# Normalising all tokens before modulating them, and projecting the last queries late, in a fused adaLN attention and feed-forward kernel

## The chip, the cores and the metric

The kernel runs on one core of a Trainium2 chip. The metric is the device time in microseconds. An execution has a few parts per thousand of scatter, so times are medians of three to eleven runs. A core has TensorE (PE in the profile, PEld for its weight loads), ScalarE (ACT), VectorE (DVE), GpSimd (POOL) and SyncE (SP, which here only issues DMA).

## The reference, cut to what matters

```python
# x: 2048 tokens x 1024, 32 heads of 32, one shared key/value head, feed-forward width 3584
mod = (silu(c) @ w_mod)                       # six rows: sa, ca, ga, sb, cb, gb
h = layernorm(x) * (1 + ca) + sa
x = x + ga * attention(h, wq, wk, wv, wo)     # softmax over 2048 keys
h = layernorm(x) * (1 + cb) + sb
x = x + gb * ((silu(h @ w1) * (h @ w3)) @ w2)
```

## The kernel before

The program builds a graph of instructions, and a list scheduler in Python orders it per engine from hand-set durations. The order on each engine is then fixed.

The queries are handled in five blocks, 256, 256, 512, 512 and 512 queries (blocks 0 to 4). In each block, attention is a stream of scores on TensorE, exponentials of 128x1024 on ScalarE (1024 in the whole kernel), and sums over values on TensorE. The score matmuls of one exponential are called a score group. The feed-forward of a block runs on TensorE, with its tanh on ScalarE, under the attention of the next block. That of block 4 runs alone at the end.

The prologue works by token blocks of 512 and interleaves them with the first attention:

```python
for tb in range(NTB):                          # 4 token blocks of 512
    for i in range(4): ln_stats(tb * 4 + i)    # VectorE
    ln_scale(tb * 4, 4)                        # GpSimd, 128x4
    for i in range(4): ln_norm(tb * 4 + i, q0 + i)         # VectorE: (x - mean) * rs
    ...
    ln_transpose(4, q0, HT of tb, ..., 0, 1, ("act", "dve") if tb < 2 else ("dve",))
                                               # TensorE transposes; the eviction from PSUM modulates
    kv(tb)
    if tb == 0: qproj(0, 0)
...
for f in range(1, NC): qproj(0, f)
...
for tb in range(1, NTB):
    for f in range(NC): qproj(tb, f)           # all queries during blocks 0 and 1
```

The softmax here doesn't subtract the row's maximum and nothing guards it: scores larger than these inputs give would overflow.

Of the kernel before, what the change touches and what calls it, by code (L numbers as in the profile page):

```python
# [8 lines left out]
P = 128  # L9
# [10 lines left out]
class Group:  # L20
    def __init__(self):
        self.bank = None
        self.nodes = []


class Dag:
# [71 lines left out]
    def schedule(self, banks):  # L98

        t_free = {e: 0.0 for e in ENGS}  # L100
# [27 lines left out]
        def free_banks():  # L128
            out = []
            for b in banks:  # L130
                if b in closed:
                    continue
                g = bank_group[b]
                if g is None:
                    out.append((0.0, b))
                elif all(x.start is not None for x in g.nodes):
                    out.append((max(x.vis for x in g.nodes), b))
            return sorted(out)

        while left:  # L140
            best = None
            for e in ENGS:
# [3 lines left out]
                fb = free_banks() if e == "pe" else None  # L146
                cands = []
                tmin = None
                for n in ready[e]:
                    est = n.est  # L150
                    if n.acq is not None:
                        if not fb:
                            continue
                        est = max(est, fb[0][0] + SEM_LAT)
# [17 lines left out]
            if e == "pe":  # L172
                att = mode in ("S", "V")

                def key(c):
                    s, n = c
                    if n.cls == "S":
                        r = 0
                    elif n.cls is not None:
                        r = 1 if att or t - n.est > 1.0 else 4  # L180
                    else:
                        r = 3
                    return (r, n.prio, n.seq)
            elif e == "dve":
                def key(c):
                    s, n = c
                    p = n.prio
                    if t - n.est > 4.0:
                        p -= 3
                    return (p, n.seq)  # L190
# [6 lines left out]
            if n.acq is not None:  # L197
                fb = free_banks()
# [123 lines left out]
def build(nc, x_in, wq_in, wk_in, wv_in, wo_in, w1_in, w3_in, w2_in, c_in, wmod_in, out, S, D, F):  # L322
# [15 lines left out]
    NTR = 5  # L338
    NXS = 8
# [16 lines left out]
    WKR = sb("WKR", [P, NC, 4, 32], BF16)  # L356
# [9 lines left out]
    RS = sb("RS", [P, NT], F32)  # L366
    NHALF = sb("NHALF", [P, 4], F32)

    HT = HREG[:].rearrange("p (c s) -> p c s", c=NC)
    HHT = HREG[:, 0:NF * 512].rearrange("p (f s) -> p f s", f=NF)  # L370
    o = NF * 512
    TS = HREG[:, o:o + 512]
    TT = HREG[:, o + 512:o + 1024]
    O2B = HREG[:, o + 1024:o + 2048].rearrange("p (a t d) -> p a t d", a=2, t=2)
    HKEY = "HREG"
# [20 lines left out]

    def grp():
        return Group()
# [21 lines left out]
    xload(0, 8)  # L420
    for k in range(NC):
        dma(lambda e, k=k: e.dma_start(WM01[:, k, :], wmod_in[k * P:(k + 1) * P, 0:2 * D]), ("wm01", k),
            writes=[("UR", k)], nbytes=P * 2 * D * 2)
    dma(lambda e: e.dma_start(WKV[:, 0], wk_in.rearrange("(c p) f -> p c f", p=P)), "wk", writes=WKK, nbytes=65536)
    dma(lambda e: e.dma_start(WKV[:, 1], wv_in.rearrange("(c p) f -> p c f", p=P)), "wv", writes=WVK, nbytes=65536)
    WQK = [("WREG", "q")]
    dma(lambda e: e.dma_start(WQ[:, :, 0:P], wq_in[:, 0:P].rearrange("(c p) f -> p c f", p=P)), "wq0",
        writes=[("WQ", 0)] + WQK, nbytes=P * D * 2)

# [16 lines left out]
    g = grp()  # L446
    for k in range(NC):
        def mm(e, k=k, g=g):
            for j in range(16):
                i = e.matmul(PB[g.bank][:, j:j + 1], WM01[:, k, j * P:(j + 1) * P], SCT[:, k:k + 1],  # L450
                             start=(k == 0 and j == 0), stop=True, skip_group_check=True)
            return i
        G.add("pe", mm, reads=["SCT", ("UR", k)], dur=16 * 0.06, lat=0.2, acq=g if k == 0 else None,
              groups=[(g, "w")], mode="F")
    G.add("dve", lambda e, g=g: e.tensor_copy(MODC[:, 0, :], PB[g.bank][:, 0:8]), writes=[("MODC", 0)],
          groups=[(g, "r")], dur=0.13, prio=0)
    G.add("dve", lambda e, g=g: e.tensor_scalar(MODC[:, 1, :], PB[g.bank][:, 8:16], 1.0, None, ALU.add),
          writes=[("MODC", 1)], groups=[(g, "r")], dur=0.13, prio=0)
    G.add("pool", lambda e: e.tensor_copy(WKR[:], WKV[:, 0].unsqueeze(2).broadcast_to([P, NC, 4, 32])), reads=WKK,
          writes=["WKR"], dur=1.3)  # L460

    def ln_stats(t):
        s, q = t % NXS, t % 4
        for a in range(2):
# [3 lines left out]
              reads=[("ST", q, 0), ("ST", q, 1)], writes=[("MV", t)], dur=0.15, prio=2)  # L468

# [7 lines left out]
    def xnt(q):  # L477

        return XN[:, q, :] if q < 4 else UREG[:, (NU + NTR - 2) * 2048 + (q - 4) * D:][:, 0:D]

    def xnk(q):
        return [] if q < 4 else [("UR", NU + NTR - 2 + (q - 4) // 2)]

    def ln_norm(t, q):
        s = t % NXS
        G.add("dve", lambda e: e.tensor_scalar(xnt(q), X[:, s, :], MV[:, t, 0:1], RS[:, t:t + 1],
                                               ALU.subtract, ALU.mult),
              reads=[("X", s), ("RS", t), ("MV", t)], writes=[("XN", q)] + xnk(q), dur=0.42, prio=2)
# [31 lines left out]

    def mm_group(n, f, reads_f, n_cols=512, per=1, prio=5, late=0):
# [13 lines left out]
    def kv(tb):  # L535
        sl = slice(tb * 512, (tb + 1) * 512)
        hk = lambda c: [("HT", c, tb), HKEY]
        g = mm_group(NC, lambda e, b, c: e.matmul(b, WKR[:, c].rearrange("p a f -> p (a f)"), HT[:, c, sl],
                                                  start=c == 0, stop=c == NC - 1), lambda c: ["WKR"] + hk(c))
        G.add("dve", lambda e, g=g: e.tensor_copy(KT[:, sl], PB[g.bank]), writes=[("KT", tb)], groups=[(g, "r")],  # L540
              dur=dve_t(512), prio=1)

        def vmm(e, b, i):
            tt, c = i // NC, i % NC
            return e.matmul(b[:, tt * 32:(tt + 1) * 32], HT[:, c, tb * 512 + tt * P:tb * 512 + (tt + 1) * P],
                            WKV[:, 1, c, :], start=c == 0, stop=c == NC - 1)
        g = mm_group(4 * NC, vmm, lambda i: WVK + hk(i % NC), n_cols=128, per=NC)
# [4 lines left out]
    def qproj(tb, f):  # L552
        sl = slice(tb * 512, (tb + 1) * 512)
        g = mm_group(NC, lambda e, b, c: e.matmul(b, WQ[:, c, f * P:(f + 1) * P], HT[:, c, sl],  # L554
                                                  start=c == 0, stop=c == NC - 1),
                     lambda c: [("WQ", min(f, 1)), ("HT", c, tb), HKEY] + WQK)
        G.add("dve", lambda e, g=g: e.tensor_copy(QT[:, f, sl], PB[g.bank]),  # L557
              writes=qkeys(f, tb * 512, 512), groups=[(g, "r")], dur=dve_t(512), prio=1)

# [3 lines left out]
    for tb in range(NTB):  # L563
        for i in range(4):
            ln_stats(tb * 4 + i)
        ln_scale(tb * 4, 4)
        q0 = 4 if tb == 1 else 0
        for i in range(4):
            ln_norm(tb * 4 + i, q0 + i)
        if tb + 2 < NTB:  # L570
            xl = xload(tb * 4 + 8, 4)
        ln_transpose(4, q0, lambda c, tb=tb: HT[:, c, tb * 512:(tb + 1) * 512],
                     lambda c, tb=tb: [("HT", c, tb)], 0, 1, ("act", "dve") if tb < 2 else ("dve",))
        kv(tb)
        if tb == 0:
            qproj(0, 0)
    dma(lambda e: e.dma_start(WQ[:, :, P:D], wq_in[:, P:D].rearrange("(c p) f -> p c f", p=P)), "wq1",
        writes=[("WQ", 1)], nbytes=7 * P * D * 2, after=xl)
    wo_load = dma(lambda e: e.dma_start(WO[:], wo_in.rearrange("(c p) f -> p c f", p=P)), "wo", writes=["WO"],
                  nbytes=D * D * 2, after=xl)  # L580
# [4 lines left out]
    def wms(i):  # L585
        return [("WMS", i)]
# [54 lines left out]
    for tb in range(1, NTB):  # L641
        for f in range(NC):
            qproj(tb, f)
# [133 lines left out]
    def post(q0, qn):  # L777
        t0, nt = q0 // P, qn // P
        npk = 512 // qn
        G.chain = 1  # L780
# [16 lines left out]
        for ft in range(NF):  # L797
            sl, sub = (ft // 2) % 2, ft % 2
            if sub == 0:
                c0 = ft * P  # L800
                for w, src in enumerate((w1_in, w3_in)):
                    dma(lambda e, c0=c0, sl=sl, w=w, src=src: e.dma_start(
                        W13[sl][w], src[:, c0:c0 + 256].rearrange("(c p) f -> p c f", p=P)),
                        ("w13", w, sl), writes=[("WR", sl, w)] + wa(w, sl), nbytes=D * 512)
# [6 lines left out]
            wk = (("WR", sl, 0), ("WR", sl, 1))  # L811
            if npk == 1:
                g1 = mm_group(NC, gmm, lambda i: [wk[0]] + qkeys(i, q0, qn), n_cols=qn)
                o1 = o3 = 0
            else:
                g1 = g3 = mm_group(2 * NC, gmm, lambda i: list(wk) + qkeys(i % NC, q0, qn), n_cols=qn)
                o1, o3 = 0, qn
            G.add("act", lambda e, g=g1: e.activation(TS[:, 0:qn], PB[g.bank][:, 0:qn], ACT.Tanh, scale=0.5),  # L818
                  writes=["TS"] + alias("TS"), groups=[(g1, "r")], dur=act_t(qn), prio=-1)
            G.add("dve", lambda e, g=g1: e.scalar_tensor_tensor(TT[:, 0:qn], TS[:, 0:qn], 1.0, PB[g.bank][:, 0:qn],  # L820
                                                                ALU.add, ALU.mult),
                  reads=["TS"], writes=["TT"] + alias("TT"), groups=[(g1, "r")], dur=dve_t(qn), prio=0)
            if npk == 1:
                g3 = mm_group(NC, lambda e, b, i, gmm=gmm: gmm(e, b, i, w0=1), lambda i: [wk[1]] + qkeys(i, q0, qn), n_cols=qn)
            G.add("dve", lambda e, g=g3, ft=ft, o3=o3: e.tensor_tensor(  # L825
                HHT[:, ft, 0:qn], TT[:, 0:qn], PB[g.bank][:, o3:o3 + qn], ALU.mult),
                reads=["TT"], writes=[("HHT", ft)] + alias(("HHT", ft)), groups=[(g3, "r")], dur=dve_t(qn), prio=0)
        for q in range(4):
# [3 lines left out]
                ("w2", r), writes=[("WR", r, w) for w in range(3)] + wa(2, r), nbytes=F * 512)  # L832
            for i0 in range(0, nt, 2):
                n = min(2, nt - i0)

                def w2mm(e, b, i, i0=i0, r=r):
# [3 lines left out]
                g = mm_group(n * NF, w2mm, lambda i, r=r: [("WR", r, w) for w in range(3)] + [("HHT", i % NF)],  # L840
# [5 lines left out]
                    reads=[("GBB", q // 2)], writes=[("O2B", ob)] + alias(("O2B", ob)), groups=[(g, "r")],  # L846
# [8 lines left out]
                for a, s0, m in runs:  # L855
# [3 lines left out]
                        reads=[("X", s0 + i) for i in range(m)] + [("O2B", ob)],  # L859
# [7 lines left out]
    first_wa = set()  # L867

    def alias(k):

        if k in first_wa:
            return []
        first_wa.add(k)
        return [HKEY]

    def wa(kind, sl):

        if (kind, sl) in first_wa:
            return []
        first_wa.add((kind, sl))  # L880
        return [("WMS", i) for i in range(3)] + WQK + [("WQ", 0), ("WQ", 1)]

    for bi, (q0, qn) in enumerate(BLOCKS):
        attention(q0, qn, bi >= FIVE, NDIR if bi else 0)
        post(q0, qn)

# [43 lines left out]
```

## Time and profile before

| | us |
|---|---|
| time, median of 3 | 1299.62 |
| first exponential starts | 38.0 |
| 65th exponential starts | 113.8 |
| last exponential ends | 1089.0 |
| from there to the end | 207.1 |

The page of the kernel before: busy time of each engine, two of the lines of 40 slices (ScalarE's tenths busy, and the granted TensorE clock in tenths), and the group of the exponentials (busy us, mean ns of one, idle before it).

```profile
PE 1177.5 (91%) x11393; PEld 583.5 (45%) x11393; DVE 877.7 (68%) x1223; ACT 1011.0 (78%) x1174; POOL 20.8 (2%) x51
...
ACT  1499999999899999989999999989999996011100
...
PEclk9898999999899999868999999999999999999999
...
L715 ACT ACTIVATE UREG<-SP 128x1024 bf16<-128x1024 f32 x1024 | 969.6, 1172 | 60.6 <-PE PB L659 32.1
```

ScalarE is the bound from about slice 3 to slice 33, but only just: TensorE is nearly as loaded. The 1172 ns of one exponential overlaps the next. Undisturbed, the stream takes 0.93 us each.

The waits of ScalarE in the kernel before, from 38 to 175 us:

```profile
ACT UREG L715 <- PE SP L704: 19.6, 9, 6.5
```

The exponentials waited 19.6 us for scores there, because keys of later token blocks were not ready. The timeline of TensorE at the end of block 2 in the kernel before (start, duration, instruction, idle before it and what ended it):

```profile
551.74 0.40 PE L704 MATMUL SP<-QT,KT 32*128 32x512 bf16 x4 [1.44 <-ACT UREG L715]
553.57 0.61 PE L704 MATMUL SP<-QT,KT 32*128 32x512 bf16 x4 [1.44 <-ACT UREG L715]
555.41 0.61 PE L704 MATMUL SP<-QT,KT 32*128 32x512 bf16 x4 [1.22 <-ACT UREG L715]
```

Four score matmuls take 0.40 us, and 0.61 us once TensorE has had little else to do for a while: the clock has been halved (the trace's clock records show half clock from 552.0 to 565.7 us). Two stretches of the kernel before, by exponentials 97 to 176 and 481 to 544 (busy time of each engine, then the mean granted clock, DMA share and GB/s):

```profile
143.20:216.70 73.50, 67.18 (x952) 29.08 (x952) 55.95 (x86) 73.35 (x81) 1.62 (x4) 1.00 0.03 8
529.00:595.30 66.30, 49.12 (x414) 16.38 (x412) 37.82 (x48) 59.25 (x66) 1.58 (x4) 0.79 0.15 43
```

In the first stretch ScalarE is busy 73.35 of 73.50 us at full clock. In the second it is idle for 7 us, at a mean clock of 0.79.

### The profile page before, as it was taken

Reading aid. Unit: us, or ns where it says so; the run is one execution under the profiler, and the core shown is the slowest. Engines: PE = TensorE matmul, PEld = TensorE weight load, DVE = VectorE, ACT = ScalarE, POOL = GpSimd, SP = SyncE. Lnnn points to the kernel's source line nnn. Section 1 sums busy time; section 2 is a strip of 40 time slices with the busy share of each in tenths; the row PEclk is TensorE's granted clock in tenths of the full one; section 3 lists DMA queues with packets and bytes.
Section 4 is the critical chain, followed back from the end, with each engine's and each line's share of the span. In section 5 each row is a group of like instructions: output and inputs, shape, how many; then the busy total and the mean of one; then the engine's idle time right before and its main releaser. Section 6 shows DMA issues by size and latency. Waiting matters only on the chain.

```text
span 1296.0 us, 26693 instructions
## 1 busy us (share of the span) xinstructions
PE 1177.5 (91%) x11393; PEld 583.5 (45%) x11393; DVE 877.7 (68%) x1223; ACT 1011.0 (78%) x1174; POOL 20.8 (2%) x51
## 2 busy tenths in 40 slices
PE   5698998899898889868999999999999999999998
PEld 3343344554455555413333335545333336754477
DVE  7888867885457787746687777656887777633421
ACT  1499999999899999989999999989999996011100
POOL 1000000000000000000000000000000000000000
PEclk9898999999899999868999999999999999999999
DMA  9533001553456556500232344202433244255563
GB/s 313 195 103 112 2 2 50 148 155 107 114 133 176 144 151 181 145 1 2 66 89 84 90 121 112 62 1 67 130 98 94 83 109 115 60 174 150 161 173 90
DMA packets 239446, 141.31 MB, mean 109 GB/s; under 512 B 6880, under 2 KB 231136, under 8 KB 239328
## 3 DMA queue, kind: packets, MB, share of 16 engines
q1 hardware_dynamic: 239328, 139.61, 37.6%
q8 instruction: 90, 1.47, 0.5%
q14 instruction: 28, 0.23, 0.1%
HBM read 135.40 MB, written 4.19 MB: 108 GB/s over the span
## 4 chain that ended last, share of the span: by engine, by line
PE 43%; ACT 41%; issue 6%; DVE 6%; DMA 3%; SPq 1%; ACTq 0%; DVEq 0%
ACT UREG L715 38%; PE PB L809 9%; PE PB L838 7%; PE SP L704 5%; PE SP L809 5%; PE PB L659 5%; PE SP L838 5%; ACT HREG L818 3%; PE PB L786 2%; DMA WREG<-in_B_w_dram 1%; DVE UREG L744 1%; PE PB L554 1%; PE PB L760 1%; DMA WREG<-in_w_mod_dram 1%; DMA UREG<-in_w_mod_dram 1%
## 5 line engine op out<-in xcount | busy, mean ns | idle before, releaser
L715 ACT ACTIVATE UREG<-SP 128x1024 bf16<-128x1024 f32 x1024 | 969.6, 1172 | 60.6 <-PE PB L659 32.1
L809 PE MATMUL PB<-QT,WREG 128*128 128x512 bf16 (+1 forms) x1904 | 361.7, 331 | 6.8 <-DVE DSB L766 2.0
L749 DVE TENSOR_TENSOR UREG<-UREG 128x2048 bf16<-128x2048 bf16 x200 | 243.2, 1216 | 31.8 <-ACT UREG L715 29.2
L704 PE MATMUL SP<-QT,KT 32*128 32x512 bf16 (+1 forms) x2560 | 207.5, 348 | 57.8 <-ACT UREG L715 44.2
L809 PEld LDWEIGHTS PB<-QT,WREG 128*128 128x128 bf16 x1904 | 166.8, 98 | 160.7 <-issue 63.3
L744 DVE TENSOR_TENSOR UREG<-UREG 128x2048 bf16<-128x2048 bf16 x100 | 121.5, 1215 | 87.3 <-ACT UREG L715 86.7
L704 PEld LDWEIGHTS SP<-QT,KT 32*128 32x128 bf16 x2560 | 54.1, 92 | 245.4 <-ACT UREG L715 231.0
L838 PE MATMUL PB<-WREG,HREG 128*128 128x256 bf16 x1232 | 152.8, 273 | 2.7 <-DVE HREG L843 1.8
L659 PE MATMUL PB<-UREG,V 128*32 128x512 bf16 (+1 forms) x2528 | 138.1, 353 | 10.2 <-DVE HREG L820 4.6
L838 PEld LDWEIGHTS PB<-WREG,HREG 128*128 128x128 bf16 x1232 | 113.1, 98 | 40.3 <-issue 24.8
L818 ACT ACTIVATE HREG<-PB 128x512 bf16<-128x512 f32 (+1 forms) x126 | 82.2, 652 | 46.9 <-PE PB L809 42.7
L769 DVE RECIPROCAL DSB<-DSB 128x128 f32<-128x128 f32 x128 | 115.1, 927 | 0.5
L820 DVE SCALAR_TENSOR_TENSOR HREG<-HREG,PB 128x512 bf16<-128x512 bf16 (+1 forms) x126 | 71.0, 563 | 45.8 <-ACT HREG L818 37.7
L659 PEld LDWEIGHTS PB<-UREG,V 128*32 128x32 bf16 x2528 | 59.2, 99 | 69.9 <-issue 25.8
L818 ACT ACTIVATE HREG<-SP 128x512 bf16<-128x512 f32 x14 | 8.4, 597 | 94.5 <-PE SP L809 94.5
L809 PE MATMUL SP<-QT,WREG 128*128 128x512 bf16 x336 | 75.0, 379 | 0.0
L554 PE MATMUL PB<-HREG,WREG 128*128 128x512 bf16 x256 | 66.2, 384 | 1.2 <-DVE QT L557 1.1
L825 DVE TENSOR_TENSOR HREG<-HREG,PB 128x256 bf16<-128x256 bf16 (+1 forms) x112 | 60.8, 543 | 5.4 <-PE PB L809 3.9
L838 PE MATMUL SP<-WREG,HREG 128*128 128x256 bf16 x560 | 62.8, 273 | 1.3 <-DMA WREG<-in_B_w_dram 1.3
L838 PEld LDWEIGHTS SP<-WREG,HREG 128*128 128x128 bf16 x560 | 54.6, 98 | 8.8 <-DMA WREG<-in_B_w_dram 1.8
L786 PE MATMUL PB<-WO,QT 128*128 128x512 bf16 x208 | 54.7, 390 | 0.1
L809 PEld LDWEIGHTS SP<-QT,WREG 128*128 128x128 bf16 x336 | 32.9, 98 | 39.4
(88 smaller groups left out, 567.0 us busy)
## 6 DMA issues: line engine op xcount, KB each, us to landing
WREG<-in_B_w_dram SPq DMA_DIRECT2D x140, 512.0 KB, 4.1
WREG<-in_B_w_dram SPq DMA_DIRECT2D x20, 1792.0 KB, 8.2
X<-in_A_x_dram SPq DMA_DIRECT2D x32, 256.0 KB, 3.7
WREG<-in_w_mod_dram SPq DMA_DIRECT2D x16, 512.0 KB, 4.9
UREG<-in_w_mod_dram SPq DMA_DIRECT2D x8, 512.0 KB, 9.1
out_dram<-X SPq DMA_DIRECT2D x16, 256.0 KB, 3.4
WO<-in_A_wo_dram SPq DMA_DIRECT2D x1, 2048.0 KB, 16.0
WREG<-in_A_wq_dram SPq DMA_DIRECT2D x1, 1792.0 KB, 11.1
```

Source lines behind the costliest of these rows:

```text
L554: g = mm_group(NC, lambda e, b, c: e.matmul(b, WQ[:, c, f * P:(f + 1) * P], HT[:, c, sl], start=c == 0, stop=c == NC - 1), lambda c: [("WQ ...
L659: r = e.matmul(PB[g.bank][32 * gg:32 * gg + 32, 0:qn], V[:, kt, :] if kind == "V" else ONES[:], U[:, pu, (gg * npk + j) * qn:(gg * npk + j ...
L704: r = e.matmul(SP[:, b, o:o + w], KT[32 * gg:32 * gg + 32, kts[j] * P:(kts[j] + 1) * P], QT[32 * gg:32 * gg + 32, f, q0 + qo:q0 + qo + w], ...
L715: G.add("act", lambda e, u=u, h0=h0, n=n, b0=b0, nb=nb, wb=wb: e.activation(U[:, u, h0 * W:(h0 + n) * W].rearrange("p (b w) -> p b w", b=n ...
L744: G.add("dve", lambda e, tr=tr, u=u, fu=first_u: e.tensor_tensor(TR[:, tr, 0:4 * W], U[:, fu, 0:4 * W], U[:, u, 0:4 * W], ALU.add), reads= ...
L749: G.add("dve", lambda e, tr=tr, u=u: e.tensor_tensor(TR[:, tr, 0:4 * W], TR[:, tr, 0:4 * W], U[:, u, 0:4 * W], ALU.add), reads=[("TR", tr) ...
L769: G.add("dve", lambda e, h=h: e.reciprocal(DSB[:, h * 128:(h + 1) * 128], DSB[:, h * 128:(h + 1) * 128]), reads=["DSB"], writes=[("DSBr", ...
L786: g = mm_group(NC, lambda e, b, f, t=t, h=h: e.matmul(b, QT[:, f, t * P:(t + 1) * P], WO[:, f, h * 512:(h + 1) * 512], start=f == 0, stop= ...
L809: return e.matmul(b[:, o:o + qn], W13[sl][w][:, c, sub * P:(sub + 1) * P], QT[:, c, q0:q0 + qn], start=c == 0, stop=c == NC - 1)
L818: G.add("act", lambda e, g=g1: e.activation(TS[:, 0:qn], PB[g.bank][:, 0:qn], ACT.Tanh, scale=0.5), writes=["TS"] + alias("TS"), groups=[( ...
L820: G.add("dve", lambda e, g=g1: e.scalar_tensor_tensor(TT[:, 0:qn], TS[:, 0:qn], 1.0, PB[g.bank][:, 0:qn], ALU.add, ALU.mult), reads=["TS"] ...
L838: return e.matmul(b[:, j * 256:(j + 1) * 256], HHT[:, fc, (i0 + j) * P:(i0 + j + 1) * P], W2S[:, r, fc, :], start=fc == 0, stop=fc == NF - 1)
```

## The change

The intent: start the exponentials late but never let them wait, by having all four token blocks normalised and transposed before them. Transposition no longer waits for the modulation columns, since modulation becomes a separate pass in place. The query projections of the last two blocks (128 of 256 matmuls of 128x512) move to block 2. To keep the transposed tokens alive that long, their layout becomes block by block, and the feed-forward's buffers move. One priority rule of the scheduler for VectorE changes too. Cut to the core:

```diff
+    def ln_stats_act(t0, n):      # token block 1: sums and squares on ScalarE with accumulation
...
+    def ln_front(tb):
+        if tb == 1: ln_stats_act(4, 4)
+        else:       (ln_stats on VectorE)
+        ...
+            ln_norm(tb * 4 + i, tb * 4 % 12 + i, "pool" if i == 3 and tb else "dve")
...
+    def ln_turn(tb, q0, engs):    # transposes, raw copies of 128x1024 from PSUM
+    def ln_modulate(tb, engs):    # in place, 128x512 each
...
+    for i in range(120):          # warm-up matmuls that nobody reads, cls="W"
...
-    for tb in range(NTB): (statistics, norm, transpose with modulation, keys and values)
+    ln_modulate(0, ("dve", "act"));  kproj(0); qproj(0, 0)
+    ln_modulate(1, ("act", "dve"));  kproj(1); vproj(0)
+    ln_modulate(2, ("dve", "pool")); kproj(2); vproj(1)
+    ln_modulate(3, ("pool", "dve")); kproj(3); vproj(2); vproj(3)
...
     for tb in range(1, NTB):
         for f in range(NC):
-            qproj(tb, f)
+            if tb not in LATE:    # LATE = (2, 3)
+                qproj(tb, f)
...
         post(q0, qn)
+        if bi == LATE_AT:         # after block 1's feed-forward, during block 2
+            late_queries(LATE)    # loads wq again, projects the last 1024 queries
```

## The prediction

> **What bounds the kernel now.** By stretches of time there are three regimes. (1) 0 to 38 us: prologue; the view by engine shows ScalarE waiting 18.9 us for the modulation columns, which wait (chain of waits) for the 4 MB of modulation weights, landed at 20.4 us. (2) 38 to 1089 us: 1024 exponentials on ScalarE. Undisturbed, 24 of them take 22.36 us (timeline), 0.93 us each; with 126 tanh ScalarE is near its bound. TensorE is nearly as loaded (about 970 us). (3) 1089 to 1296 us: the last feed-forward, TensorE only, over 99% busy.
>
> ScalarE does not run at full rate from 38 us: the waits view has it waiting 19.6 us for scores between 38 and 175 us (longest 6.5), because keys of token blocks 1 to 3 are not ready. The 65th exponential starts at 113.8 us; at 0.93 us each the stream behaves as if it had begun at 54.3 us.
>
> **What the change does.** All statistics, normalisation and transposes come before the first exponential; modulation is a separate in-place pass. Added: 8 statistics passes and 10 copies of 128x1024 on ScalarE (estimate 1.1 us each, from the 1.17 us exponential), 8 modulations there (0.7 us each, as the 128x512 evictions), 16 on VectorE, 8 on GpSimd, 120 dummy matmuls. All precede the first exponential in ScalarE's order. The modulation columns move from 21 us to after the last modulation weights, which now queue behind x: estimate 35 to 37 us. Token block 3 (load, statistics, GpSimd normalisation, transpose, copy) ends at about 38 us. Then eight modulations, key and query projection, scores: first exponential at 45 us (estimate; 40 to 50), 7 us later than before, but then continuous, since the four key blocks are needed only every 3.7 us. Effective start about 47 instead of 54.3: 7 us won.
>
> **Moved work.** 128 query matmuls (27.6 us at 0.216) leave TensorE in blocks 0 and 1, where ScalarE was the bound anyway: nothing won. They land at the end of block 2, where the timeline shows TensorE nearly idle: 541 to 566 us. There scores take 0.61 us instead of 0.39 and the value batch 1.90 instead of about 1.05: half clock. The Trainium skill, "TensorE: Matmul & The Clock Gate", Part 1, says that the clock halves after an idle activity window; this trace agrees. ScalarE loses about 5.4 us between 545 and 576 us. Filled with projections most of it returns: 3 us won, less a little for 16 evictions (0.69 us) on VectorE. But the hole moves: at the end of block 0 about 19 score groups (35 us) now have no other TensorE work; the clock should halve there, costing about 3 us. Blocks 3, 4 and the last feed-forward are unchanged.
>
> **Predicted: 1292 us**, range 1281 to 1303. Faster by over 2%: 0.03; within 2%: 0.95; slower: 0.02.
>
> **What would show it.** First exponential near 45 us, the 65th near 106; ScalarE waits for scores before 175 us below 6 us; a new stretch of half clock between about 135 and 180 us; full clock between 530 and 570 us; unchanged length from the last exponential to the end (207 us).
>
> **What would make it wrong.** The small-packet key and value weights, now first in the queue, delay x; ScalarE passes with accumulation or GpSimd passes cost twice the estimate (first exponential past 50 us: no gain or a loss); or VectorE, with the late evictions, holds up the sums in block 2. A prologue that ends at 38 us would give 1284.

## The result, and the profile after

The changed kernel takes 1309.35 us (median of 4) against 1299.07 us (the table above has one run less). The ratio is 1.0073, with a 95% interval of 1.0056 to 1.0091. Ratios here and below are the mean time of one kernel's fast runs over that of the other's of the same rounds, so they are not quite the ratio of the medians quoted. The predicted 1292 and its range are missed: the change made the kernel slower, by 0.7%.

The page of the changed kernel, the lines that answer to those of before:

```profile
PE 1180.5 (90%) x11424; PEld 594.5 (45%) x11513; DVE 875.5 (67%) x1206; ACT 1029.8 (79%) x1200; POOL 43.2 (3%) x73
...
ACT  5699989999889999989899999988999996011100
...
PEclk7897968999899999999999999999999999999999
...
L846 ACT ACTIVATE UREG<-SP 128x1024 bf16<-128x1024 f32 x1024 | 970.4, 1181 | 59.1 <-PE PB L790 40.2
```

The same exponentials, with the same total of waiting, so the totals do not tell where the time went. The start of each exponential does. The table has its lag behind the same exponential of the kernel before, in us (start in the trace minus start in the trace of before, numbered from 0):

| exponential | 0 | 64 | 192 | 480 | 640 | 832 | 1023 |
|---|---|---|---|---|---|---|---|
| before, start | 38.0 | 113.8 | 233.2 | 529.0 | 695.8 | 889.5 | 1087.6 |
| changed, lag | +15.5 | +4.4 | +10.2 | +8.7 | +7.4 | +11.3 | +11.3 |

After the last exponential both need 207 us. So there are three losses: 4.4 us by the 64th, 5.8 us between the 64th and the 192nd, and 3.9 us between the 640th and the 832nd. Two small gains, together 2.8 us, lie between.

**The first loss.** The chain of work that led to the first exponential of the changed kernel (start, duration, what):

```profile
37.54 4.08 POOL XN L523
...
44.04 7.13 DVE HREG L612 x11
...
53.58 1.02 ACT UREG L846
```

One normalisation on GpSimd takes 4 us, and eleven modulations on VectorE take 7 us. The normalisations in the prologue of the changed kernel by engine (minimum, median and maximum ns, first and last start):

```profile
L523 DVE TENSOR_SCALAR UREG<-X,MV,RS x6: 529/546/1431, 20.3 to 24.3; 128x1024 bf16<-128x1024 bf16 x6
L523 POOL TENSOR_SCALAR UREG<-X,MV,RS x2: 3781/3786/3792, 24.2 to 28.0; 128x1024 bf16<-128x1024 bf16 x2
L523 POOL TENSOR_SCALAR XN<-X,MV,RS x1: 4071/4071/4071, 37.5 to 37.5; 128x1024 bf16<-128x1024 bf16 x1
```

The same instruction takes 0.55 us on VectorE and 3.8 to 4.1 us on GpSimd. The first of the three also held up a load: a buffer of x that GpSimd has not yet read can't be loaded with the next tokens, so a load of x was issued only at 28.1 us, when that normalisation had ended at 28.0. The last modulation weights are queued behind it and landed at 35.8 us. They were not what the columns waited for in the end: on TensorE the last matmuls of the columns are ordered behind the transposes of the last normalised tokens, and the columns were there at 44.0 us.

**The second loss.** The waits of ScalarE in the changed kernel from 125 to 215 us, where the same view of the kernel before lists none:

```profile
ACT UREG L846 <- PE SP L835: 4.7, 6, 1.3
```

The timeline of TensorE in the changed kernel, in that stretch:

```profile
168.18 0.61 PE L835 MATMUL SP<-QT,KT 32*128 32x256 bf16 x8 [1.22 <-ACT UREG L846]
170.02 0.61 PE L835 MATMUL SP<-QT,KT 32*128 32x256 bf16 x8 [1.22 <-ACT UREG L846]
171.02 1.90 PE L790 MATMUL PB<-UREG,V 128*32 128x256 bf16 x32 [0.39 <-DVE UREG L880]
```

This is the picture that the end of block 2 had before: only scores and sums, at half clock. But the waits are not the whole of the 5.8 us. From the 64th to the 192nd exponential ScalarE waited 4.7 us, against 0.8 before, and it also did eight tanh of the feed-forward there instead of two. In the run without GpSimd below, a tanh of 128x256 sets the stream back by about 0.2 us (three exponentials and a tanh take 2.97 us). That work is only moved: 20 follow up to the 320th instead of 26. The two stretches of the changed kernel, exponentials 97 to 176 and 481 to 544:

```profile
147.80:227.70 79.90, 58.35 (x926) 28.45 (x929) 51.34 (x79) 75.13 (x85) 1.62 (x4) 0.79 0.13 36
537.70:602.20 64.50, 57.80 (x459) 19.53 (x464) 42.17 (x54) 58.97 (x66) 0.79 (x2) 0.97 0.15 42
```

The clock of 0.79 has moved from the second stretch to the first. The first became 6.4 us longer, while the second became only 1.8 us shorter. Why so little is in the timeline of the changed kernel:

```profile
555.74 4.49 PE L677 MATMUL PB<-HREG,WREG 128*128 128x512 bf16 x20
...
560.16 1.91 PE L790 MATMUL PB<-UREG,V 128*32 128x512 bf16 x32
560.83 25.77 ACT L846 ACTIVATE UREG<-SP 128x1024 bf16<-128x1024 f32 x28 [4.55 <-PE PB L790]
```

Twenty query matmuls were ordered in one run, and the value sums, which free the exponentials' buffers, stand behind them. ScalarE waits 4.55 us. Its waits from 500 to 620 us, first in the kernel before, then in the changed one:

```profile
ACT UREG L715 <- PE SP L704: 5.4, 4, 1.8
ACT UREG L715 <- PE PB L659: 3.6, 4, 1.6
...
ACT UREG L846 <- PE PB L790: 4.8, 2, 4.6
ACT UREG L846 <- PE SP L835: 1.0, 2, 0.7
```

So the waits for scores did go, and waits for value sums came in their place. From the 480th to the 640th exponential these rose from 6.2 to 11.3 us.

### The profile page after: what moved, and what is told of

It is laid out like the page before. It is cut to its first block, busy times and chain, and to the rows that moved or that the text cites. A ratio compares the mean times of both kernels' runs of the same rounds, so it can differ in the third digit from the quotient of the medians.

```text
span 1307.5 us, 26890 instructions
## 1 busy us (share of the span) xinstructions
PE 1180.5 (90%) x11424; PEld 594.5 (45%) x11513; DVE 875.5 (67%) x1206; ACT 1029.8 (79%) x1200; POOL 43.2 (3%) x73
## 4 chain that ended last, share of the span: by engine, by line
ACT 43%; PE 41%; issue 7%; DVE 5%; DMA 1%; POOL 0%; SPq 0%; ACTq 0%; DVEq 0%
ACT UREG L846 40%; PE PB L943 9%; PE PB L972 7%; PE SP L835 5%; PE SP L943 5%; PE PB L790 5%; PE SP L972 5%; ACT WKR L952 3%; PE PB L920 2%; DVE UREG L875 1%; PE PB L891 1%; PE SP L920 1%; PE PB L677 1%; DVE UREG L880 1%; DMA WREG<-in_B_w_dram 1%
## 5 line engine op out<-in xcount | busy, mean ns | idle before, releaser
L943 PE MATMUL PB<-QT,WREG 128*128 128x512 bf16 (+1 forms) x1861 | 358.1, 331 | 22.2 <-issue 6.0
L952 ACT ACTIVATE WKR<-PB 128x512 bf16<-128x512 f32 (+1 forms) x126 | 85.1, 676 | 44.5 <-PE PB L943 41.6
L954 DVE SCALAR_TENSOR_TENSOR WKR<-WKR,PB 128x512 bf16<-128x512 bf16 (+1 forms) x126 | 70.7, 561 | 44.8 <-ACT WKR L952 40.6
L952 ACT ACTIVATE WKR<-SP 128x512 bf16<-128x512 f32 x14 | 8.4, 597 | 94.5 <-PE SP L943 94.5
L959 DVE TENSOR_TENSOR HREG<-WKR,PB 128x256 bf16<-128x256 bf16 (+1 forms) x112 | 60.5, 540 | 4.6 <-PE PB L943 3.2
L677 PE MATMUL PB<-HREG,WREG 128*128 128x512 bf16 x233 | 58.3, 381 | 2.4 <-issue 1.4
```

Of the source, the lines that this page charges most:

```text
L677: g = mm_group(NC, lambda e, b, c: e.matmul(b, w[:, c, :], HT[:, c, tb], start=c == 0, stop=c == NC - 1), lambda c: wkeys + htk(c, tb), la ...
L943: return e.matmul(b[:, o:o + qn], W13[sl][w][:, c, sub * P:(sub + 1) * P], QT[:, c, q0:q0 + qn], start=c == 0, stop=c == NC - 1)
L952: G.add("act", lambda e, g=g1: e.activation(TS[:, 0:qn], PB[g.bank][:, 0:qn], ACT.Tanh, scale=0.5), writes=["TS"], groups=[(g1, "r")], dur ...
L954: G.add("dve", lambda e, g=g1: e.scalar_tensor_tensor(TT[:, 0:qn], TS[:, 0:qn], 1.0, PB[g.bank][:, 0:qn], ALU.add, ALU.mult), reads=["TS"] ...
```

## The experiments

Two theories stood at first. *G*: GpSimd spoils the prologue. *H*: late queries leave a hole at the end of block 0 in which the clock halves. Their rivals were the queue of loads (R1), and a knock-on of the prologue (R2). All kernels below gave correct results. Lags are against the kernel before, as above, each from one profiled execution. The times of one kernel scatter by up to some us, so a lag at the end can be off from the medians by as much; the lengths of single stretches repeat better (see the step below).

| run | median us | ratio to before, 95% | lag at 0 | 64 | 192 | 480 | 640 | 832 |
|---|---|---|---|---|---|---|---|---|
| changed | 1309.35 | 1.0073, 1.0056 to 1.0091 | +15.5 | +4.4 | +10.2 | +8.7 | +7.4 | +11.3 |
| e2_no_gpsimd | 1299.99 | 1.0010, 0.9994 to 1.0027 | +6.8 | -3.9 | +1.2 | -0.9 | -2.2 | +1.7 |
| e3_no_late | 1307.49 | 1.0060, 1.0047 to 1.0073 | +15.0 | +3.4 | +8.9 | +9.7 | +9.0 | +9.0 |
| e4_late_only | 1305.69 | 1.0048, 1.0036 to 1.0060 | -0.3 | +0.7 | +6.5 | +2.3 | +1.8 | +5.6 |
| e4c_layout_only | 1297.53 | 0.9989, 0.9977 to 1.0001 | -0.2 | +1.0 | +1.3 | +0.4 | -0.1 | -0.1 |
| e5_nogp_nolate | 1290.62 | 0.9939, 0.9924 to 0.9953 | +6.8 | -4.8 | -5.9 | -7.0 | -7.7 | -7.7 |
| e6_nogp_late3 | 1295.77 | 0.9975, 0.9963 to 0.9986 | +6.4 | -5.1 | -2.2 | -4.4 | -3.3 | -3.3 |
| e7_hole_filled | 1292.39 | 0.9950, 0.9935 to 0.9966 | +6.8 | -3.2 | -2.3 | -9.5 | -9.2 | -5.3 |
| e9_gp_muladd | 1303.40 | 1.0031, 1.0018 to 1.0045 | +9.6 | -2.7 | +3.0 | +3.3 | +2.8 | +6.7 |
| e1_norm_dve | 1299.90 | 1.0007, 0.9993 to 1.0020 | +7.5 | -3.3 | +1.7 | -0.5 | -1.6 | +2.2 |
| e11_warm_blk2 | 1288.34 | 0.9918, 0.9904 to 0.9932 | +6.4 | -5.4 | -6.4 | -7.7 | -15.0 | -11.2 |
| e12_nogp_late2 | 1294.08 | 0.9962, 0.9949 to 0.9976 | +7.3 | -3.3 | -1.8 | -4.0 | -3.7 | -3.7 |
| e13_no_warm | 1290.18 | 0.9940, 0.9923 to 0.9957 | +6.6 | -5.4 | -6.5 | -7.7 | -7.9 | -7.9 |
| e14_warm_nospill | 1288.37 | 0.9922, 0.9906 to 0.9938 | +7.0 | -5.1 | -6.2 | -7.4 | -9.9 | -9.9 |
| e15_late3_warm | 1292.71 | 0.9947, 0.9935 to 0.9960 | +7.0 | -5.4 | -2.4 | -6.5 | -4.0 | -4.0 |

**e2_no_gpsimd: no normalisation or modulation on GpSimd.**

```diff
-            ln_norm(tb * 4 + i, tb * 4 % 12 + i, "pool" if i == 3 and tb else "dve")
+            ln_norm(tb * 4 + i, tb * 4 % 12 + i, "dve")
-    ln_modulate(2, ("dve", "pool"))
+    ln_modulate(2, ("dve",))
-    ln_modulate(3, ("pool", "dve"))
+    ln_modulate(3, ("dve",))
```

> The changed kernel with all three GpSimd normalisations and all eight GpSimd modulations given to VectorE; the queries stay late. Theory G (GpSimd is what spoils the prologue: in the trace its three normalisations took 3.8 to 4.1 us each against my estimate of 1.1, and while it modulated, VectorE's modulations took 0.86 us each instead of 0.40): the first exponential comes at 45 to 48 us instead of 53.6, and the time falls by 5 to 8 us, to about 1302 (ratio 1.002). Rival R1 (the prologue is late because the modulation weights queue behind the loads of x, whichever engine normalises): the first exponential stays within 2 us of 53.6 and the time at 1308.

The first exponential came at 44.8 us, and the median fell by 9.4 us against the changed kernel, both a little more than expected. G holds, and R1 falls. The loss by the 64th exponential (+4.4) became a gain (-3.9), which is 8.3 of the 11.3 us. It is also the 45 us of the prediction's first exponential, and the chain is the predicted one: columns at 36.2 us, the first copy of the last token block done at 37.4, eight modulations on ScalarE in 5.6 us, then keys and scores. So the prediction's sum was right except for what GpSimd costs. The hole is still there: from the 64th to the 192nd, 5.1 us are lost again.

**e3_no_late: all queries early.**

```diff
-    LATE = (2, 3)
+    LATE = ()
```

> The changed kernel with its new prologue, but all queries projected early as before. Theory H (late queries leave a hole of about 19 score groups at the end of block 0 in which TensorE's clock halves and ScalarE waits): no half clock between 145 and 182 us, exponentials 128 to 192 no later against the kernel before than the 64th (plus 4 to 5 us instead of plus 10), but the half clock returns near 545 to 570 us; net 2 to 4 us faster than the changed kernel, about 1305. Rival R2 (the loss between exponentials 96 and 176 comes from the prologue's knock-on, not from the queries): the lag still grows to 10 us there.

Half a hit. The lag stays at +3.4 to +4.6 up to the 176th exponential, where the changed kernel loses 6.6 us, so H holds and R2 falls. But then 4.3 us are lost within 16 exponentials, and the total was 1307.5 where I had said 1305. The queries hold the buffer that the feed-forward's first weights load into. With this late prologue the queries end so late that three of those loads were issued only at 225.7 to 227.4 us and landed between 229.7 and 234.5 us, and the first feed-forward matmul came at 233.1 us, with waits of ScalarE of 1.2 to 2.6 us around it. So late queries seem to have a use that I had not seen: they free a buffer sooner. This is read from the trace; no run tests it alone.

**e4_late_only and its control e4c_layout_only: the old prologue in the new memory layout, with and without late queries.** The edit puts the loop of the kernel before, quoted above, in the place of the new prologue, with its order of loads and VectorE priorities. In the control, `LATE = ()` as well.

> The late queries alone: the prologue of the kernel before, in the new memory layout. Theory H: the first exponential at 38 us as before, a half-clock hole before block 1 that costs 5 to 7 us, a gain of about 3 us between 500 and 620 us; together 2 to 4 us slower than before, ratio 1.002 to 1.003. Rival R2 (late queries harmless): ratio 0.998 to 1.000.

> Control: neither the new prologue nor the late queries, only the new memory layout with its finer dependencies. Both theories expect the time before within 0.15%, ratio 0.999 to 1.001. If it is off by more, the layout is a third cause.

The layout costs nothing (0.9989). Late queries by themselves cost 0.59% between these two, about 7.7 us, which is more than I had expected. From the 64th to the 192nd exponential 5.8 us are lost, as in the changed kernel. A part is won back by the 480th. At the end of block 2, where the gain was meant to be, only 0.5 us is won. Between 640 and 832 there is again the step of 3.8 us, which nothing had predicted.

**e5_nogp_nolate: both undone.** The edits of e2 and e3 together.

> New prologue without GpSimd normalising or modulating, and all queries early. If the parts add up as the lags of the single runs say (prologue 4 us ahead of the kernel before at the 64th exponential, then the step of 4 us near exponential 180 that the run without late queries showed while it waited for the first feed-forward weights): about the time before, 1297 to 1299. If that step belonged to the late prologue and goes with it: 1294 to 1295.

1290.6 us, better than both branches of the expectation. The step near exponential 180 went with the late prologue, which fits queries that now end early enough for the feed-forward's weights. This is the changed kernel without the GpSimd passes and without late queries, and it beats the kernel before by 0.61%.

**e6_nogp_late3: only the last 512 queries late.**

```diff
-    LATE = (2, 3)
+    LATE = (3,)          # on top of e2's edits
```

> New prologue without GpSimd, and only the last 512 queries late (64 matmuls instead of 128). The hole of block 0 shrinks from 20 score groups to 5 and no query matmul is left for block 3. Theory H with its second part (query matmuls that spill into block 3, 19 in the changed kernel, 4.1 us, push a TensorE-bound stretch and cost that much between exponentials 704 and 832): lag against before stays at minus 4 through the 176th exponential, no step between 704 and 832, a gain near 500 to 540; about 1293, ratio 0.995 to 0.997. Rival R3 (late queries cost whatever their number): ratio 1.000 or more.

The step between 704 and 832 is gone. But 4 us were still lost between exponentials 128 and 176. Not all of that is the hole, which is now five score groups: ScalarE waited 2.3 us for scores, and four tanh of the feed-forward had moved in front of the 176th exponential (none in e5). At the end of block 2 nothing was won: from the 480th to the 640th 1.1 us were lost. So 1295.8, 5 us slower than with all queries early.

**e7_hole_filled: more work in the hole.**

```diff
             if tb not in LATE:
                 qproj(tb, f)
+    for j in range(12):   # 96 matmuls that nobody reads, on top of e2's edits
+        mm_group(NC, lambda e, b, c, j=j: e.matmul(b, IDENT[:], HT[:, c, 2 + j % 2], ...), ...)
```

> The run without GpSimd with 96 more matmuls that nobody reads (identity against the transposed tokens) in the hole at the end of block 0. In order no hole of four score groups is left, but 48 query matmuls instead of 19 now spill into block 3. Theory H: more work on TensorE makes the stretch from exponential 96 to 176 5 to 6 us shorter than in the run without GpSimd (no half clock there); and the step between 704 and 832 grows from 4 to about 10 us. Rival R2 (the hole costs for another reason than the clock): the stretch from 96 to 176 stays as long or grows.

This is the direct test of H. The stretch of exponentials 97 to 176 in the run without GpSimd:

```profile
139.20:218.60 79.40, 57.66 (x928) 28.57 (x928) 51.31 (x79) 75.02 (x85) 1.59 (x4) 0.79 0.13 35
```

and with 96 matmuls more in the hole:

```profile
139.90:215.30 75.40, 70.15 (x994) 32.72 (x998) 48.93 (x76) 74.39 (x83) 1.59 (x4) 0.95 0.12 31
```

TensorE does 12.5 us more, and the stretch is 4.0 us shorter (I had said 5 to 6), at a clock of 0.95 instead of 0.79. Over 64 to 192 the loss falls from 5.1 to 0.9 us; of these 4.2, 3.2 are waits of ScalarE for scores (4.2 to 1.0 us), and two tanh fewer lie in the stretch. Useless work that makes a stretch faster can only act through the clock or through a changed order, and the clock moved as expected. The whole kernel is 7.6 us faster, but only 4.2 us of that lie here. Another 5.1 us came between the 192nd and the 480th, where the order differs too; they are not explained. Elsewhere 2.3 us were lost. The second expectation failed: the step between 704 and 832 stayed at 3.9 us, although 48 query matmuls spilled into block 3 instead of 19.

**e9_gp_muladd: GpSimd normalises by multiply and add.**

```diff
-  tensor_scalar(xn, x, mean, rs, ALU.subtract, ALU.mult)
+  tensor_scalar(xn, x, rs, nmr, ALU.mult, ALU.add)      # nmr = -mean * rs, two tiny GpSimd steps before
```

> The changed kernel, with GpSimd normalising by multiply and add (scale, and minus mean times scale) instead of subtract and multiply. GpSimd modulates 128x512 by multiply and add in 0.79 us, so 128x1024 should take 1.6 us. Theory S (the operation, not the engine, made the three normalisations take 3.8 us): they take 1.5 to 1.8 us and the first exponential comes about 4 us earlier, near 49. Rival (width, source or destination makes it slow): still 3.8 us, no change.

The three normalisations of this run:

```profile
L529 POOL TENSOR_SCALAR UREG<-X,RS,NMR x2: 1188/1191/1194, 24.8 to 26.8; 128x1024 bf16<-128x1024 bf16 x2
L529 POOL TENSOR_SCALAR XN<-X,RS,NMR x1: 1207/1207/1207, 35.9 to 35.9; 128x1024 bf16<-128x1024 bf16 x1
```

1.19 us instead of 3.79, and less than the 1.5 to 1.8 expected: same engine, width, type, source and destination, other operations (and so other columns of scalars). The first exponential came at 47.7 us, and the lag at the 64th fell by 7.1 us. So it was the pair subtract and multiply that made GpSimd slow. Which of the two it is stays open.

**e1_norm_dve: only the normalisations moved off GpSimd**, the first edit of e2.

> The changed kernel with only the three GpSimd normalisations given to VectorE; GpSimd still modulates. Splits the 8.3 us that the prologue lost at the 64th exponential: with multiply and add on GpSimd it was 7.1 us better than changed, with no GpSimd at all 8.3 us. Expected: lag at the 64th exponential minus 2.5 to minus 3.5 against before, 1301 to 1303; VectorE's modulations still 0.86 us each while GpSimd modulates. If the lock between the two engines were the larger part, the lag would stay above plus 1.

1299.9, below the 1301 to 1303 expected, and as without any GpSimd. So the eight GpSimd modulations cost at most about 0.6 us at the 64th exponential. They do block VectorE: in the changed kernel, while GpSimd modulated,

```profile
L612 DVE TENSOR_SCALAR HREG<-HREG,MODC x11: 395/856/857, 44.0 to 50.8; 128x512 bf16<-128x512 bf16 x11
```

and in the run without GpSimd

```profile
L612 DVE TENSOR_SCALAR HREG<-HREG,MODC x24: 403/407/415, 36.2 to 47.6; 128x512 bf16<-128x512 bf16 x24
```

One modulation takes 0.86 us against 0.41: in the changed kernel's trace the two engines take turns, one every 0.78 us. The Trainium skill, "SBUF — State Buffer", section "Who interferes with whom", says that a VectorE instruction in a two-port mode shares a pair of ports with GpSimd, held for a whole instruction by whichever comes first, with the other fully blocked. This trace agrees in that the two alternate. But with the normalisations gone the order changed too. My expectation that VectorE's modulations would all stay at 0.86 us failed: their median in this run was 0.41.

**e13_no_warm: 1 warm-up matmul instead of 120**, on top of e5.

> The fastest kernel so far with 1 instead of 120 warm-up matmuls at the start. Its clock was halved again from 16 to 30 us with the 120, well before the first projections at 37 us, so I expect no change: 1290 to 1291, first exponential within 0.5 us of 44.8. Rival: the warm-up matters for the transposes, and the first exponential comes 1 to 2 us later.

No difference (0.9940 and 0.9939). The warm-up matmuls are useless where they stand: in e5 the clock records show full clock from 6.2 to 16.5 us and half clock again until 30.1.

**e11_warm_blk2: useless work where the late queries were**, on top of e5.

```diff
         post(q0, qn)
+        if bi == LATE_AT:        # 80 matmuls that nobody reads, after block 1's feed-forward
+            for j in range(10): mm_group(NC, lambda e, b, c: e.matmul(b, IDENT[:], KT[:, ...], ...), ...)
```

> The fastest kernel so far (new prologue without GpSimd passes, all queries early, 1290.6) with 80 matmuls that nobody reads at the end of block 2, where the late queries stood. Theory H (what the late queries gain there is only a TensorE kept busy and so at full clock): the lag against the run without them falls by 3 to 5 us between exponentials 512 and 640, half clock near 535 to 560 us gone; about 1286 to 1288. Rival (the gain of the late queries came from the lighter block 0 and 1): no change, or slower by the work added.

Exponentials 481 to 544 without these matmuls (e5):

```profile
522.00:586.60 64.60, 47.00 (x414) 16.03 (x413) 37.84 (x48) 59.27 (x66) 1.56 (x4) 0.84 0.15 45
```

and with them:

```profile
521.30:579.80 58.50, 55.44 (x471) 20.42 (x475) 34.34 (x41) 58.50 (x66) 0.77 (x2) 1.00 0.16 48
```

At full clock the stretch is 6.1 us shorter and ScalarE is never idle. So the place was worth about 7 us up to the 640th exponential, of which the late queries got 0.5 to 1.3. But then 3.8 us are given back between 640 and 832: the step, in a kernel with no late query at all.

**e12_nogp_late2: block 3's own queries late instead of block 4's**, `LATE = (2,)` on top of e2.

> As the run with only the last 512 queries late, but block 3's own queries (1024 to 1535) late instead of block 4's. In order nothing spills into block 3. The step of 3.9 us between exponentials 704 and 832 was there with 19 and with 48 query matmuls spilled, and absent with none. If it comes with any spill, it is absent here and the time is as with the last 512 late, 1295 to 1297. If it comes with block 3's own queries being late, it is here and the time is 1299.

No step, 1294.1. So the step does not come from block 3's own queries being late. It was there in every run in which some extra matmuls were ordered after the last scores of block 2 (19 in the changed kernel, e1, e2, e4 and e9, 32 in e11, 48 in e7), and in none without. (The 26 of the expectation below counts e11's from one score group later. The traces of the changed kernel, e1 and e11 lack a few per cent of the matmul records and show 17, 17 and 29.)

**e14_warm_nospill and e15_late3_warm: useless work at the end of block 2 without a spill.** e11 with 6 groups instead of 10; and e6 with 4 such groups (32 matmuls) after its late queries.

> As the fastest kernel so far (80 unread matmuls at the end of block 2, of which 26 in order come after the last scores of block 2), but 48, all before them. Theory X (any extra matmul spilled into block 3 sets its feed-forward 16 to 18 matmuls behind the exponentials, and that is paid as 3.9 us between exponentials 704 and 832): no step there, gain of 3 to 6 us between 480 and 640 kept, 1285 to 1287. Rival Y (whatever the exponentials win at the end of block 2 is paid back, because TensorE is the bound between 704 and 832): a step of about the size of the gain, 1289 to 1291.

> The run with only the last 512 queries late (1295.8) with 32 unread matmuls after them, none spilled into block 3, so that the hole left before block 3 is filled. Theory X: the gain between 480 and 640 grows from about 0 to 2 to 4 us and no step follows between 704 and 832; 1292 to 1294. Rival Y: the gain is paid back, 1295 to 1297.

In neither is there a step (-9.9 stays -9.9, -4.0 stays -4.0), so the spill goes with the loss, and payback by a TensorE-bound stretch (Y) falls. The gain at the end of block 2 was smaller than I had said for e14, 2.5 us against 3 to 6, and its time of 1288.4 lies between the two expectations, so it is the lags that decide. Half clock came back right after the filler: in e14 from 552.2 to 555.6 and from 559.1 to 565.9 us. For e15 the part from 480 to 640 was a loss of 2.5 us, and what its trace won against e6's lay before the 480th, so there only the missing step was foreseen. (These two traces are only 0.7 us apart, the medians 3.1.) e14 is level with e11: about a third of the gain against e5 by the 640th exponential, but nothing given back.

What the spill does can be read from the traces. In e11, 23 of the extra matmuls ran after the 512th exponential had started. At the 640th exponential 197 matmuls of block 2's feed-forward were done in e2, e4, e7 and e9, and 213 in e5 and e14 (the traces of the other runs with a step lack some records). The 16 that are missing are one of the feed-forward's 28 tiles, with its tanh. That work then falls into exponentials 704 to 832, where TensorE was busy 120.4 of 124.8 us before, and 123.0 of 128.6 us in the changed kernel.

Why the step is 3.8 to 3.9 us for 19 and for 48 spilled matmuls alike can be read too: from exponential 512 to 900 ScalarE has one fixed order in all nine kernels without the step, and another in all seven with it. In the second the last tanh of block 2 comes after exponential 723 instead of 718. From exponential 640 to 832 the nine take 193.7 us each, with 15 tanh and 9.7 us of waits for value sums. The seven take 197.5 us each, with 16 tanh and 13.0 us of waits. So a spill of any of these sizes turned the schedule by one tile. That the turned order alone, without a spill, would cost the same was not tested.

## Why the prediction was wrong

- **The bound, and the worth of the prologue: right.** "First exponential at 45 us" and a gain there held once GpSimd was out (44.8 us, along the predicted chain). But "then continuous" was too good: the 65th exponential came at 109.0 us in e5, not at 106, with 5.6 us of waits of ScalarE for scores before it, so 4.8 us were won instead of 7.
- **"8 on GpSimd", "GpSimd normalisation": mis-sized, and the largest miss.** This is the step that failed: token block 3 was to end "at about 38 us", with eight modulations after it and the first exponential at 45. The prediction gave GpSimd no figure of its own; the expectation of e2 says that 1.1 us stood behind it, and the scheduler had 1.2 us set. (A GpSimd copy of 128x1024 takes 1.04 us in the trace before.) A normalisation took 3.8 to 4.1 us. The last one ran from 37.5 to 41.6 us in the chain, the columns came at 44.0 us instead of 35 to 37, and the first exponential at 53.6. Shown by e1 and e9 (7.7 and 7.1 us at the 64th exponential), and named only in the last paragraph as what might go wrong.
- **"The hole moves ... costing about 3 us": right in mechanism and place** (half clock for 23.9 of the 27.3 us from 154.5 to 181.8 us; predicted 135 to 180), mis-sized: 5.1 to 5.8 us are lost there, of which some 4 are waits for scores and most of the rest tanh that came earlier. Shown by e7.
- **"Filled with projections most of it returns: 3 us won": wrong in size.** 1.3 us in the changed kernel and 0.5 in e4, against about 7 that the place was worth (e11). The waits for scores did go, 5.4 to 1.0 us, but the projections themselves held up the value sums: a fixed run of 20 matmuls alone put a wait of 4.55 us there.
- **"Blocks 3, 4 ... are unchanged": wrong.** 3.9 us were lost there in every kernel with matmuls spilling out of block 2. Shown by e12, e14 and e15 against e2, e7 and e11.
- **"A small delay of x by the small-packet weights"** came, but small: the first tile of x landed at 5.7 us instead of 4.0.

With the measured sizes the sum is +4.4, +5.8, -2.8 and +3.9, that is +11.3 us, the lag of the last exponential. The sum of the prediction was -7, +3, -3 and 0. The prologue's term alone missed by more than the whole gain that was forecast.

## What to carry to other kernels

Before giving an instruction to GpSimd to relieve VectorE, look for that very instruction, with its operations, in a trace: a copy is no measure for it, and a slow helper at the end of a chain of loads can cost its whole duration. Work taken from an engine that is not the bound may cost time: here what was left of it ran at half clock, so look at the granted clock where the work was, not only where it goes. And see whether a filler runs over into the next block: here every such run paid 3.8 us there, whatever its size.

## What the Trainium skill lacked or had wrong

- No page gives GpSimd's time for a tensor_scalar by its pair of operations. "GPSIMD Engine Reference" counts elementwise work in cycles per element, without this case. Measured, 128x1024 bf16 with two pointer scalars: subtract and multiply 3.79 us, multiply and add 1.19 us.
- "TensorE: Matmul & The Clock Gate", Part 1, ties the halved clock to an idle window of 3.4 us, and its section on oscillation asks for no idle gap longer than that. A later section there tells that short idle gaps can do it too, without a number. In the changed kernel the clock halved while no gap was longer than 1.44 us: from 150.8 us score groups of 0.40 us came every 1.84 us, and at 154.5 us one took 0.61. The durations agree with the page's window: in the clock records of all runs every half-clock stretch but the last, which the end cuts off, lasts a whole number of 3.41 us (in the changed kernel 3.4, 6.8, 10.2, 17.1 or 20.5).
- "SBUF — State Buffer", section "Who interferes with whom", agrees with the trace (0.86 against 0.41 us for a VectorE modulation while GpSimd modulates), but says nothing of what it costs a kernel: here at most about 0.6 us at the 64th exponential, with that VectorE work in another order.
